# Empty rows of a sorted buffer written from 16 partitions and asked ahead of a weight load

## The chip, the cores and the metric

The kernel runs on one core of a Trainium2 chip. The metric is the device time of one launch in microseconds (us), taken as the median of several runs. The engines are named as the profile names them: PE is TensorE's matmuls, DVE is VectorE, ACT is ScalarE, POOL is GpSimd, SP is SyncE. Loads and stores are asked by SP's queue (q1) or by POOL's (q0); both are carried by the core's 16 DMA engines.

## What is computed

Three layers follow each other: an attention between 8 x 8 heads of 512 tokens and 32 state rows, a gated product layer, and a mixture of 8 experts with one expert for each token. Only the last matters here:

```python
def _moe2_ref(x, w_gate, w_output_gate, w1, w2):   # x: 4352 x 512 here
    logits = x @ w_gate
    e_idx = np.argmax(logits, axis=1)
    ...
    for e in range(E):                             # 8 experts
        mask = e_idx == e
        h = np.maximum(x[mask] @ w1[e], 0.0)       # 512 -> 1024
        ye = h @ w2[e]                             # 1024 -> 512
        out[mask] = gate_w[mask, None] * eom[mask, e, None] * ye
```

How many tokens an expert gets is known only on the chip. All matrix products are done with each operand split into a high and a low part.

## The kernel before

**Stages.** The first 700 us compute the first two layers, a group of 544 tokens at a time, and for each finished group the router's numbers. POOL then scatters the group's rows (L224) into a buffer in device memory, `ysort`, of 4 x 36864 rows of 130 numbers: 128 values, a gate, and the token's number. Each expert has its own stretch of rows in it, filled from the front; `cum` counts them. When the last 256 tokens are being computed, most rows are sorted, and the expert that has most of them (`eoh`, chosen by `choose`) is known, so two steps of 256 of its rows are run ahead of the others, in an order written out by hand in `moe_kernel`. Behind them comes a loop (`run`, L1278 on) whose steps are read from a table that the chip has made by then; every engine runs its own program in it, and all engines enter it together, when everything ahead of it is finished, transfers too.

**Empty rows.** A step works on 256 rows, or 128 for a half step's transfer, so the last step of an expert reads past its last row. What stands there must be harmless: zeros, with a number (`PADID`) beyond the last token, which makes the store leave the row out. `pads` (L1060) writes 128 such rows behind each expert's last row, and 128 more for the chosen expert, nine blocks in all, each into the four quarters of `ysort`. The places are in `pad`, worked out in `table` (L1135 to L1143). The source is `zrow`, one empty row on each of the 128 partitions.

**The order around it.** On SP's queue there stand, in the order of the source: the first two fetches of rows (`fetch_pre`), the load of the next expert's second weight into `raw2` (`load_rank`, L1093, which needs the expert's number from `rtab`), the nine writes of `pads`, and the third fetch (`fetch_pre(2)`), which reads `ysort` and so waits for every row written to it, by POOL or by `pads`. ACT and DVE split `raw2` into its high and low part in four quarters (`wsplit(1, raw2, c)`, L903 and L904) between their copies of the products' results (L964 relu copies, L970). Between the third and the fourth quarter DVE turns the third fetch's data (`turn(0)`, L946), and `parts` (L955, L961) splits it for the loop's first step. `pin` keeps the order of the source on PE, ACT, DVE and SP in this part.

**Stores.** The two steps ahead of the loop give their result to `preout` (L1054): DVE scales (L980), POOL writes rows by their token numbers (L990). Both stores of a step write to `out`; the scheduler knows no more of the places, so the second waits for the first. For writes that it is told are disjoint (`disjoint`, used by the scatter and by `pads`) it makes no such wait.

Of the kernel before, what the change touches and what calls it, by code (L numbers as in the profile page):

```python
# [8 lines left out]
F32 = mybir.dt.float32  # L9
F32R = mybir.dt.float32r  # L10
I32 = mybir.dt.int32
# [7 lines left out]
P = 128  # L19
# [14 lines left out]
RB = DM // 4 + 2  # L34
YW = 16 * RB
PADID = 1 << 20
# [774 lines left out]
ds = bass.ds  # L811
# [4 lines left out]
HB = 64  # L816
# [6 lines left out]
class Phase2:  # L823
# [82 lines left out]
    def tiles(self, ctx):  # L906
        tc, ph = self.tc, self.ph
        p = ctx.enter_context(tc.tile_pool(name="m1", bufs=1, reuse_waits="tile"))
        self.raw2 = p.tile([P, 4 * CH], F32, name="raw2")
        self.yT = p.tile([P, 4, 2, G], F32R, name="yT")  # L910
        self.hT = p.tile([P, 2, 2, 2, G], F32R, name="hT")
        self.hTB = self.hT.rearrange("p j f h n -> p (j f h n)").rearrange("p (c h n) -> p c h n", c=8, h=2)
        self.yts = p.tile([P, CH], F32, name="yts")
        self.hs = ph.srT.rearrange("p j n -> p (j n)")
        self.tab = p.tile([1, NSTEP, len(FIELDS)], I32, name="tab")
        self.zrow = p.tile([P, RB], F32, name="zrow")
        self.nc.gpsimd.memset(self.zrow[:, 0 : RB - 1], 0.0)
        self.nc.gpsimd.memset(self.zrow[:, RB - 1 : RB].bitcast(I32), PADID)
        self.ob = [ph.yTf[:, F2 + DM * i : F2 + DM * i + DM] for i in range(2)]
        bank = lambda pool, tag, n: pool.tile([P, 512], F32, tag=tag, name=n)  # L920
        self.ps_h = [bank(ph.ps_ab, "ab", f"ps_h{i}") for i in range(2)]
        self.ps_o = [bank(ph.ps_y, f"y{i}", f"ps_o{i}") for i in (2, 3, 0, 1)]
# [131 lines left out]
    def preout(self, k):  # L1054
        for t in range(2):
            self.gate(self.nc.vector, k, t)
            self.store(self.nc.gpsimd, k, t)

    def pads(self):

        nc = self.nc
        why = "table() bounds every field"
        _, rows = nc.values_load_multi_w_load_instructions(
            self.pad[0:1, 0 : NE + 1],
            engines=[nc.sync.engine],
            min_val=0,
            max_val=NE * CAP - P,
            skip_runtime_bounds_check_because=why,
        )
        for row in rows:  # L1070
            i = nc.sync.dma_start(
                out=self.ph.ysort[:, ds(row, P), :].rearrange("a p w -> p a w"),
                in_=self.zrow.unsqueeze(1).to_broadcast([P, 4, RB]),
            )
            self.ph.disjoint(i)

    def load(self, e, k, *names):

        why = "table() bounds every field"
        i = AT[names[0]]  # L1080
        lim = [LIMIT[n] for n in names]
        _, v = self.nc.values_load_multi_w_load_instructions(  # L1082
            self.tab[0:1, k, i : i + len(names)],
            engines=[e.engine],
            min_val=0,
            max_val=max(lim),
            skip_runtime_bounds_check_because=why,
        )
        return [
            self.nc.s_assert_within(x, int(n in ("rank1", "rank")), m, skip_runtime_bounds_check_because=why)  # L1090
            for x, m, n in zip(v, lim, names)
        ]
# [6 lines left out]
    def table(self, cp):  # L1099
# [6 lines left out]
        def t(shape, dt=F32):  # L1106
            n = 1
            for d in shape:
                n *= d
            o = tmp[:, free[0] : free[0] + n]  # L1110
            free[0] += n
            if len(shape) == 2:
                o = o.rearrange("p (a b) -> p a b", a=shape[0])
            return o.bitcast(dt)

        def iota(shape, pattern, base=0, cm=0):
# [10 lines left out]
            out=lt, in_=lt, pattern=[[1, NE], [-1, NE]], compare_op=ALU.is_gt, fill=0.0, base=0, channel_multiplier=0  # L1127
# [16 lines left out]
        self.fold = self.ph.tri[:, 0 : P // 2]  # L1144
        x, y = (self.ph.ident[:, P // 2 * i : P // 2 * i + P // 2] for i in range(2))
        nc.gpsimd.tensor_tensor(out=self.fold, in0=x, in1=y, op=ALU.add)

        yield
        V.scalar_tensor_tensor(out=cnt, in0=self.eoh, scalar=float(-G * NPRE), in1=cnt, op0=ALU.mult, op1=ALU.add)
# [15 lines left out]
        def red(o, i):  # L1165
# [3 lines left out]
            out=cmp, in0=key.unsqueeze(1).to_broadcast(sq), in1=key.unsqueeze(2).to_broadcast(sq), op=ALU.is_gt  # L1169
# [11 lines left out]
        er = pick(e8)  # L1181
        V.tensor_copy(out=self.rtab, in_=er)
        self.load_rank()
        self.pads()
        yield
        nr = pick(nb)
        gr = pick(ng)
# [19 lines left out]
        def total(o, v, scalar, op0, u=None):  # L1207
# [8 lines left out]
        rank, row, fst, lst, ex2, ex1, bsr, ngr, at, over = (t([1]) for _ in range(10))  # L1216
# [4 lines left out]
            out=later[:, 0:NE], in0=er, scalar=float(-NE), in1=ex[:, 0:NE], op0=ALU.add, op1=ALU.mult  # L1221
# [39 lines left out]
            out=own,  # L1261
# [8 lines left out]
            out=ps[:, 0:n], lhsT=self.ph.ones, rhs=own.rearrange("p k f -> p (k f)"), start=True, stop=True  # L1270
# [111 lines left out]
    def pool(self, guard):  # L1382
        e, s = self.nc.gpsimd, self.s

        def store(k):
            def both():
                for t in range(2):
                    e.wait_ge(s["o"], 2 * (k + 1) + t + 1)
                    self.store(e, k, t).then_inc(s["so"], 16)

            def half():

                e.wait_ge(s["so"], 32 * (k + 1))
                self.store(e, k, 1, HB, self.zrow[:, RB - 1 : RB]).then_inc(s["so"], 16)
                e.wait_ge(s["o"], 2 * (k + 2))
                self.store(e, k, 0, HB).then_inc(s["so"], 16)

            if k < 0:
                both()
                return  # L1400
            (kind,) = self.load(e, k, "half")
            with e.If(kind == 0):
                both()
            with e.Else():
                half()

        def fetch(k):
            half, row = self.load(e, k, "half", "row")
            if k > 3:
                e.wait_ge(s["tn"], k - 3)  # L1410

            def go(n):
                for d in self.fetch(e, self.yin[k % 3], self.gt[k % 4], row, n):
                    d.then_inc(self.sy[k % 3], 16)

            with e.If(half == 0):
                go(2)
            with e.Else():
                go(0)

        fetch(1)
        fetch(2)

        def step(k):
            store(k - 1)
            guard(k + 2, lambda: k and fetch(k + 2))

        def end(k):
            store(k)
            e.wait_ge(s["so"], 32 * (k + 2))  # L1430

        guard.run(step, end)
# [336 lines left out]
def moe_kernel(tc, x, state, w_a, w_b, w_out, w_gate, w_og, w1, w2, out):  # L1769
    w_a, w_b, w_out = (w.bitcast(I32) for w in (w_a, w_b, w_out))  # L1770
    with ExitStack() as ctx:
# [10 lines left out]
        w2 = lambda c: m.wsplit(0, m.raw1[:, 1], c)  # L1782
        turn = lambda i: m.turn(tc.nc.vector, m.yin[i])
        stage = lambda: next(table, None)
        turn(0)
        m.parts()
# [78 lines left out]
```

## Time and profile before

| | us |
|---|---|
| three runs | 1182.05, 1184.09, 1184.73 |
| median | 1184.09 |
| profiled execution | 1187.72 |
| its span | 1186.0 |
| PE busy | 1123.9 (95%) |
| DVE busy | 648.5 (55%) |
| ACT busy | 430.1 (36%) |
| POOL busy | 283.9 (24%) |

The profile is one execution; its span is the time between the first and the last instruction, and all moments below are counted from its start. A timeline has the start and the duration of an instruction, or of several alike (x4) from the first's start to the last's end; the brackets have how long the engine had been idle and what released it. A releaser called "issue" means that the profile shows none. The waits of a queue are totals, with their number and the longest. A row of a table by windows has the length of the window, the busy time of PE, PEld (weight loads), DVE, ACT and POOL, the clock that TensorE was granted (1.00 is full), the share of the 16 DMA engines that was busy (transfers can overlap, so it can pass 1) and the GB/s that they moved. Issues of DMA on SP are not busy time, and what a transfer costs from the ask to its landing stands in a list of its own.

### The profile page before, as it was taken

Reading aid. Unit: us, or ns where it says so; the run is one execution under the profiler, and the core shown is the slowest. Engines: PE = TensorE matmul, PEld = TensorE weight load, DVE = VectorE, ACT = ScalarE, POOL = GpSimd, SP = SyncE. Lnnn points to the kernel's source line nnn. Section 1 sums busy time; section 2 is a strip of 40 time slices with the busy share of each in tenths; the row PEclk is TensorE's granted clock in tenths of the full one; section 3 lists DMA queues with packets and bytes.
Section 4 is the critical chain, followed back from the end, with each engine's and each line's share of the span. In section 5 each row is a group of like instructions: output and inputs, shape, how many; then the busy total and the mean of one; then the engine's idle time right before and its main releaser. Section 6 shows DMA issues by size and latency. Waiting matters only on the chain. (4 is left out here: it accounts for less than half of the span.)

```text
span 1186.0 us, 19358 instructions
## 1 busy us (share of the span) xinstructions
PE 1123.9 (95%) x7032; PEld 902.4 (76%) x7032; DVE 648.5 (55%) x1118; ACT 430.1 (36%) x706; POOL 283.9 (24%) x392
## 2 busy tenths in 40 slices
PE   3898999999999999999999999969999999999994
PEld 1665777777677777776777799859899998889983
DVE  5889646565464465654754366742442444455463
ACT  4765424333333343333432245321421324142341
POOL 2000005006023050060230524311331232232121
PEclk8898999999999999999999999989999999999997
DMA  6563320302203103020000116369271253536420
GB/s 196 192 226 107 72 38 30 79 3 72 38 15 78 19 30 79 1 72 1 12 26 1 35 33 182 96 128 239 67 204 41 62 166 74 147 89 164 103 97 21
DMA packets 102497, 98.92 MB, mean 83 GB/s; under 512 B 60144, under 2 KB 76048, under 8 KB 102352
## 3 DMA queue, kind: packets, MB, share of 16 engines
q1 hardware_dynamic: 90920, 71.56, 23.2%
q0 software_dynamic: 11168, 25.52, 7.6%
q8 instruction: 72, 1.18, 0.4%
q14 instruction: 73, 0.60, 0.2%
q10 hardware_dynamic: 264, 0.07, 0.0%
HBM read 76.75 MB, written 21.15 MB: 83 GB/s over the span
## 5 line engine op out<-in xcount | busy, mean ns | idle before, releaser
L1009 PE MATMUL ps_h<-yT,w 128*128 128x256 f32 x1536 | 197.5, 285 | 11.0 <-issue 10.0
L1009 PEld LDWEIGHTS ps_h<-yT,w 128*128 128x128 f32 x1536 | 193.9, 193 | 16.8 <-issue 10.8
L1030 PE MATMUL ps_o<-w,hT 128*128 (+1 forms) x768 | 188.1, 394 | 2.3 <-DVE hT L970 2.2
L224 POOL DMA_INDIRECT ysort<-y,gdu x136 | 152.2, 1119 | 149.4 <-DVE y L797 105.8
L528 PE MATMUL ps_y<-gh,wo_h 128*128 128x512 f32 (+1 forms) x432 | 167.1, 392 | 2.1 <-ACT wo_h L218 1.9
L528 PE MATMUL ps_y<-gh,wo_l 128*128 128x512 f32 (+1 forms) x432 | 165.5, 383 | 0.1
L1030 PEld LDWEIGHTS ps_o<-w,hT 128*128 128x128 f32 x768 | 141.5, 190 | 29.8 <-issue 2.4
L528 PE MATMUL ps_y<-gl,wo_h 128*128 128x512 f32 (+1 forms) x432 | 163.3, 379 | 0.0
L516 PE MATMUL ps_ab<-Ah,Mh 128*128 128x512 f32 x384 | 129.6, 418 | 6.8 <-ACT Mh L258 6.8
L501 DVE TENSOR_TENSOR a<-a,ps_ab 128x512 f32<-128x512 f32 x96 | 65.6, 684 | 127.8 <-PE ps_ab L516 126.9
L516 PE MATMUL ps_ab<-Al,Mh 128*128 128x512 f32 x384 | 121.8, 398 | 0.0
L516 PE MATMUL ps_ab<-Ah,Ml 128*128 128x512 f32 x384 | 119.5, 392 | 0.0
L516 PEld LDWEIGHTS ps_ab<-Ah,Mh 128*128 128x128 f32 x384 | 66.7, 191 | 63.1 <-issue 40.2
L990 POOL DMA_INDIRECT out<-yT,gt x37 | 44.6, 1205 | 281.6 <-DVE yT L980 226.7
L964 ACT ACTIVATE hT<-ps_h 128x512 fp32r<-128x512 f32 x64 | 38.0, 593 | 201.5 <-PE ps_h L1009 194.1
L258 ACT ACTIVATE gh<-a 128x512 fp32r<-128x512 f32 (+1 forms) x108 | 65.4, 606 | 106.5 <-DVE a L501 106.5
L528 PEld LDWEIGHTS ps_y<-gh,wo_h 128*128 128x128 f32 x432 | 81.6, 189 | 26.5 <-issue 6.3
L259 DVE TENSOR_TENSOR gl<-a,gh 128x512 fp32r<-128x512 f32 (+1 forms) x108 | 71.1, 658 | 44.6 <-ACT gh L258 44.5
L970 DVE SCALAR_TENSOR_TENSOR hT<-ps_h,hT 128x512 fp32r<-128x512 f32 x64 | 44.0, 687 | 93.7 <-ACT hT L964 93.7
L500 ACT ACTIVATE a<-ps_ab 128x512 f32<-128x512 f32 x96 | 57.5, 599 | 101.4 <-PE ps_ab L516 101.2
L528 PEld LDWEIGHTS ps_y<-gl,wo_h 128*128 128x128 f32 x432 | 81.5, 189 | 16.3
L259 DVE TENSOR_TENSOR Ml<-ps_m,Mh 128x512 fp32r<-128x512 f32 x96 | 61.8, 684 | 56.5 <-ACT Mh L258 56.5
(255 smaller groups left out, 1410.7 us busy)
## 6 DMA issues: line engine op xcount, KB each, us to landing
raw<-in_moe_w SPq DMA_DIRECT2D x32, 512.0 KB, 10.1
raw<-in_moe_w SPq DMA_DIRECT2D x8, 2048.0 KB, 9.6
x<-in_x SPq DMA_DIRECT2D x7, 1024.0 KB, 5.5
xin<-in_x SPq DMA_DIRECT2D x96, 64.0 KB, 2.6
y<-in_moe_w_a SPq DMA_DIRECT2D x8, 512.0 KB, 5.8
yT<-in_moe_w_b SPq DMA_DIRECT2D x8, 512.0 KB
y<-ysort POOLq DMA_DIRECT2D x28, 128.0 KB, 8.6
y<-in_moe_w_out SPq DMA_DIRECT2D x6, 512.0 KB, 5.5
```

Source lines behind the costliest of these rows:

```text
L224: self.disjoint(self.nc.gpsimd.indirect_dma_start(**kw))
L258: self.nc.scalar.activation(out=hi, in_=src, func=AF.Copy)
L259: self.nc.vector.tensor_tensor(out=lo, in0=src, in1=hi.bitcast(F32), op=ALU.subtract)
L500: nc.scalar.activation(out=a[:, 0:n], in_=pa[:, 0:n], func=AF.Copy)
L501: nc.vector.tensor_tensor(out=a[:, 0:n], in0=a[:, 0:n], in1=pb[:, 0:n], op=ALU.mult)
L516: nc.tensor.matmul(out=ps, lhsT=m[:, ab, q, c0 : c0 + P], rhs=r[:, q, :], start=i == 0, stop=i == 5)
L528: nc.tensor.matmul(out=y, lhsT=l[:, f, P * c : P * c + P], rhs=r, start=f == 0 and i == 0, stop=f == NFC - 1 and i == 2,)
L964: return e.activation(out=self.hT[:, j % 2, :, 0, :], in_=self.ps_h[j % 2].rearrange("p (f n) -> p f n", f=2), func=AF.Relu)
L970: return e.scalar_tensor_tensor(out=l, in0=self.ps_h[j % 2].rearrange("p (f n) -> p f n", f=2), scalar=0.0, in1=h.bitcast(F32), op0=ALU.ma ...
L990: return e.indirect_dma_start(out=self.out, out_offset=bass.IndirectOffsetOnAxis(ap=to[0:rows].bitcast(U32), axis=0), in_=self.ob[t][0:row ...
L1009: m = e.matmul(out=self.ps_h[j % 2][:, G * (f % 2) : G * (f % 2) + G], lhsT=self.w1[:, wh, x : x + P], rhs=self.yT[:, c, yh, :], start=k == 0,
L1030: m = e.matmul(out=self.ps_o[2 * (k % 2) + t], lhsT=self.hT[:, j % 2, f, hh, P * t : P * t + P], rhs=self.w2c(slot, wh, 2 * j + f), start= ...
```

## The change

The empty rows get another source and another place in the queue, and two stores lose a wait.

- `tiles` makes no `zrow`. It clears the first 1040 columns of the first 16 partitions of `raw1`'s slot 0, which w1's splits are done with by then, and puts `PADID` into every 130th of them: 16 x 8 empty rows. A one-column `padid` takes over what the loop's half steps read from `zrow`.
- Each write of `pads` takes 8 rows in a run from each of 16 partitions, 64 pieces of 4160 bytes, where it took one row from each of 128, 512 pieces of 520 bytes.
- `pads` is called in `table` right behind the counts, one stage earlier, ahead of `load_rank`.
- `preout` tells the scheduler that its stores are disjoint.

```diff
@@ tiles
-        self.zrow = p.tile([P, RB], F32, name="zrow")
-        self.nc.gpsimd.memset(self.zrow[:, 0 : RB - 1], 0.0)
-        self.nc.gpsimd.memset(self.zrow[:, RB - 1 : RB].bitcast(I32), PADID)
+        self.padid = p.tile([P, 1], F32, name="padid")
+        self.nc.gpsimd.memset(self.padid.bitcast(I32), PADID)
+        self.empty = self.raw1[0:16, 0, 0 : 8 * RB]
+        self.nc.gpsimd.memset(self.empty, 0.0)
+        ids = self.empty.rearrange("p (r w) -> p r w", r=8)[:, :, RB - 1 : RB]
+        self.nc.gpsimd.memset(ids.bitcast(I32), PADID)
@@ preout
-            self.store(self.nc.gpsimd, k, t)
+            self.ph.disjoint(self.store(self.nc.gpsimd, k, t))
@@ pads
-                out=self.ph.ysort[:, ds(row, P), :].rearrange("a p w -> p a w"),
-                in_=self.zrow.unsqueeze(1).to_broadcast([P, 4, RB]),
+                out=self.ph.ysort[:, ds(row, P), :].rearrange("a (p r) w -> p a (r w)", p=16),
+                in_=self.empty.unsqueeze(1).to_broadcast([16, 4, 8 * RB]),
@@ table
         nc.gpsimd.tensor_tensor(out=self.fold, in0=x, in1=y, op=ALU.add)
+        self.pads()
 
         yield
...
         self.load_rank()
-        self.pads()
         yield
@@ pool, store, half
-                self.store(e, k, 1, HB, self.zrow[:, RB - 1 : RB]).then_inc(s["so"], 16)
+                self.store(e, k, 1, HB, self.padid).then_inc(s["so"], 16)
```

On SP's queue, between the second fetch and the third, this stood before (raw_6994 is `raw2`, raw_6148 is `raw1`; DMAHW0 to 7 are eight counters that the transfers of this queue take in turn, DMASW0 to 7 those of POOL's queue, and a transfer whose counter is still in use waits for it):

```order
L1096 TENSOR_LOAD rtab [waits DVE_49]
...
L894 DMA raw_6994<-in_moe_w 128x8x512 [waits DMAHW6_49,DVE_49]
L1063 TENSOR_LOAD pad
...
L1071 DMA ysort<-zrow 128x4x130 [waits DMAHW4_49,DMAHW3_49,DMAHW5_49,DMAHW2_49,DMAHW7_49,DMAHW1_49,Pool_49]
...
L1071 DMA ysort<-zrow 128x4x130 [waits DMAHW0_49]
...
L1071 DMA ysort<-zrow 128x4x130
...
L1071 DMA ysort<-zrow 128x4x130 [waits DMAHW6_49]
...
L1071 DMA ysort<-zrow 128x4x130 [waits DMAHW7_49]
L941 TENSOR_LOAD esel
...
L932 DMA y<-ysort 32x8x128 [waits DMAHW0_49,DMAHW7_49,DMASW1_49,DVE_49]
```

and this stands there now:

```order
L1066 TENSOR_LOAD pad [waits DVE_49]
...
L1074 DMA ysort<-raw_6148 16x4x1040 [waits DMAHW4_49,DMAHW5_49,DMAHW3_49,DMAHW6_49,DMAHW2_49,DMAHW7_49,DMAHW1_49,Pool_49]
...
L1074 DMA ysort<-raw_6148 16x4x1040
...
L1074 DMA ysort<-raw_6148 16x4x1040 [waits DMAHW0_49]
...
L1074 DMA ysort<-raw_6148 16x4x1040
...
L1074 DMA ysort<-raw_6148 16x4x1040 [waits DMAHW6_49]
L1099 TENSOR_LOAD rtab [waits DVE_49]
...
L894 DMA raw_6994<-in_moe_w 128x8x512 [waits DMAHW7_49,DVE_49]
L944 TENSOR_LOAD esel
...
L935 DMA y<-ysort 32x8x128 [waits DMAHW0_49,DMAHW6_49,DMASW1_49,DVE_49]
```

The nine writes have moved ahead of `raw2`'s load, whose counter is now the one of the second write (DMAHW7), so that it waits for that write's landing; the third fetch stays last.

On POOL, behind the last scatter of the group before and ahead of the rank sums of the last tokens (`cum`), the empty row is written. Before:

```order
L760 COPY y<-ids 128x8
L917 MEMSET zrow 128x129 [waits DVE_49]
L918 MEMSET zrow 128x1
L748 TENSOR_TENSOR cum<-cum,goh 128x8 [waits DVE_49,PE_49,Pool_49]
L747 COPY gpre<-cum 128x8 [waits Pool_49]
```

and now:

```order
L760 COPY y<-ids 128x8
L917 MEMSET padid 128x1 [waits DVE_49]
L919 MEMSET raw_6148 16x1040 [waits DMAHW3_49,DMAHW4_49,DMAHW2_49,DMAHW5_49,DMAHW1_49,DMAHW6_49,DMAHW0_49,DMAHW7_49,DVE_49,PE_49]
L921 MEMSET raw_6148 16x8 [waits Pool_49]
L748 TENSOR_TENSOR cum<-cum,goh 128x8 [waits DVE_49,PE_49]
L747 COPY gpre<-cum 128x8 [waits Pool_49]
```

The clearing now waits for SP's loads and for the splits of w1, since its place is a piece of `raw1`; its position on POOL is the same. The two early stores on POOL lie behind the scatters of the last tokens. Before:

```order
L1146 TENSOR_TENSOR tri<-ident 128x64 [waits PE_49]
L224 DMA ysort<-y,gdu 147456x130 [waits DMAHW4_49,DMAHW3_49,DMAHW5_49,DMAHW2_49,DMAHW6_49,DMAHW1_49,DMAHW7_49,DMASW2_49,DVE_49]
...
L224 DMA ysort<-y,gdu 147456x130 [waits DMASW1_49]
L990 DMA out<-yT,gt_6499 4352x512 [waits DMASW2_49,DMAHW0_49,DVE_49,Activation_49]
L990 DMA out<-yT,gt_6499 4352x512 [waits DMASW3_49,DMASW2_49,DVE_49]
```

and now:

```order
L1149 TENSOR_TENSOR tri<-ident 128x64 [waits PE_49]
L224 DMA ysort<-y,gdu 147456x130 [waits DMAHW4_49,DMAHW3_49,DMAHW5_49,DMAHW2_49,DMAHW6_49,DMAHW1_49,DMAHW7_49,DMASW2_49,DVE_49]
...
L224 DMA ysort<-y,gdu 147456x130 [waits DMASW1_49]
L993 DMA out<-yT,gt_6499 4352x512 [waits DMASW2_49,DVE_49,Activation_49]
L993 DMA out<-yT,gt_6499 4352x512 [waits DMASW3_49,DVE_49]
```

The second store no longer waits for the first (DMASW2), and the first no longer for a transfer of SP's queue (DMAHW0). On PE nothing moves, and on ACT and DVE only the counter of `raw2`'s load is another.

## Rows read from the trace of the kernel before

**Rows 1.** TensorE timeline: start us, us, line, operation, count, [idle before, releaser].

```profile
784.96 2.91 PE L1030 MATMUL ps_o<-w,hT 128*128 128x512 f32 x12
797.87 4.49 PE L1009 MATMUL ps_h<-yT,w 128*128 128x256 f32 x24 [10.00 <-issue]
```

**Rows 2.** Windows: us, PE, PEld, DVE, ACT, POOL, clock, DMA share, GB/s.

```profile
790.00:792.00 2.00, 0.00 (x0) 0.00 (x0) 0.89 (x1) 0.00 (x0) 0.00 (x0) 0.69 0.03 1
```

**Rows 3.** Waits of the SyncE queue, 720 to 800: total us, times, longest.

```profile
SPq L932 <- DMA ysort<-zrow: 7.3, 1, 7.3
SPq L1322 <- DVE w L904: 4.5, 1, 4.5
```

**Rows 4.** SyncE timeline: the w2 load, the empty rows, the third fetch.

```profile
761.68 0.40 SPq L894 DMA_DIRECT2D raw<-in_moe_w  x1
763.32 13.76 SPq L1071 DMA_DIRECT2D ysort<-zrow  x9
785.55 2.06 SPq L932 DMA_DIRECT2D y<-ysort  x4
```

**Rows 5.** VectorE timeline: counts, w2 splits (L904), copy (L970), turn (L946).

```profile
754.05 0.17 DVE L1143 CAST pad<-srT 128x9 int32<-128x9 f32 x1
777.08 1.21 DVE L904 TENSOR_TENSOR w<-raw,w 128x1024 fp32r<-128x1024 f32 x1
778.22 0.43 DVE L1272 CAST tab<-ps_tab 1x280 int32<-1x280 f32 x1
780.17 0.69 DVE L970 SCALAR_TENSOR_TENSOR hT<-ps_h,hT 128x512 fp32r<-128x512 f32 x1 [1.53 <-ACT hT L964]
781.12 2.36 DVE L904 TENSOR_TENSOR w<-raw,w 128x1024 fp32r<-128x1024 f32 x2 [0.26 <-ACT w L903]
791.11 1.25 DVE L946 STREAM_TRANSPOSE yts<-y 128x1024 f32<-128x1024 f32 x1 [7.63 <-DMA y<-ysort]
794.51 1.23 DVE L904 TENSOR_TENSOR w<-raw,w 128x1024 fp32r<-128x1024 f32 x1 [0.17 <-ACT w L903]
```

**Rows 6.** DMA issues: count, KB each, median us from ask to landing.

```profile
raw<-in_moe_w SPq DMA_DIRECT2D x8, 2048.0 KB, 9.6
ysort<-zrow SPq DMA_DIRECT2D x9, 260.0 KB, 10.2
```

**Rows 7.** Windows during empty rows, a 128-partition w2 load, a 32-partition w1 load.

```profile
775.00:776.00 1.00, 1.00 (x7) 0.86 (x6) 0.93 (x13) 0.00 (x0) 0.72 (x1) 1.00 1.23 183
...
882.00:883.00 1.00, 1.00 (x11) 1.00 (x10) 0.81 (x2) 0.00 (x0) 0.00 (x0) 1.00 1.07 410
...
948.00:949.00 1.00, 1.00 (x7) 0.84 (x6) 0.00 (x0) 0.82 (x1) 0.00 (x0) 1.00 1.06 205
```

**Rows 8.** SyncE line L1063: count, duration ns min, median, max.

```profile
L1063 SPq TENSOR_LOAD <-pad x1: 793/793/793, 762.1 to 762.1; - x1
```

**Rows 9.** POOL timeline: memset, rank sums, last scatter, second early store.

```profile
734.11 0.21 POOL L917 MEMSET zrow<- 128x129 f32 x1 [7.49 <-DVE wl L259]
751.42 0.20 POOL L748 TENSOR_TENSOR cum<-cum,goh 128x8 f32<-128x8 f32 x1 [17.07 <-DVE goh L733]
764.22 0.98 POOL L224 DMA_INDIRECT ysort<-y,gdu  x1 [0.30 <-issue]
785.07 0.98 POOL L990 DMA_INDIRECT out<-yT,gt  x1 [9.35 <-issue]
```

**Rows 10.** ScalarE timeline: first split of raw2, relu copies (L964).

```profile
773.64 1.05 ACT L903 ACTIVATE w<-raw 128x1024 fp32r<-128x1024 f32 x1
779.54 0.60 ACT L964 ACTIVATE hT<-ps_h 128x512 fp32r<-128x512 f32 x1 [4.85 <-PE ps_h L1009]
785.16 0.60 ACT L964 ACTIVATE hT<-ps_h 128x512 fp32r<-128x512 f32 x1 [3.12 <-PE ps_h L1009]
```

**Rows 11.** SyncE timeline in the loop: a w2 load, four w1 loads.

```profile
877.26 0.40 SPq L894 DMA_DIRECT2D raw<-in_moe_w  x1
944.42 1.82 SPq L897 DMA_DIRECT2D raw<-in_moe_w  x4
```


## The prediction

> **What bounds the kernel now.** I read four views of the seam between the hand-ordered steps and the last loop, in this order: TensorE's timeline for the hole, the waits of the SyncE queue for its cause, the timelines of SyncE, VectorE and ScalarE for the chain that ends it, and the DMA rates for what each load costs.
>
> [...] The reader sees "issue" as the releaser, which here is the common start of the loop on all engines. Who is last to it is told by the SyncE queue: it waits 4.5 us for VectorE's w at L904, and before that its fetch at L932 waits 7.3 us for the empty rows, ysort<-zrow [rows 3]. So the chain is: raw2 asked at 761.68, nine transfers of empty rows asked from 763.32 on over 13.76 us, the third fetch released at 785.55 [rows 4], its data turned by VectorE from 791.11, the last w2 split over at 795.74 (794.51 + 1.23) [rows 5], the loop at 797.87, which is 2.13 us later. Everything from the turn to the end of that split takes 4.63 us.
>
> The queue works in order, and sizes and rates reproduce this. A 2048 KB w2 load takes 9.6 us from ask to landing; nine times 260 KB are 2.40 MB of empty rows [rows 6]; while they run alone the DMA moves 183 GB/s [rows 7]. So 761.7 + 9.6 + 2.40 MB / 183 GB/s (13.1 us) = 784.4 against the release seen at 785.5. I use the same reckoning below.
>
> **The change part by part.**
>
> *The ask moves ahead.* The counts are in pad at 754.22 (754.05 + 0.17) [rows 5]. Loading them into registers takes SyncE 0.79 us [rows 8], and before the first transfer followed 1.2 us after that load began (763.32 against the end of raw2's issue at 762.08). So the first empty rows are asked at about 755.5, 7.8 us earlier. Nine issues go at the pace of the fetch (four in 2.06 us, about 0.55 us each with its register work) [rows 4], 5 us in all, hidden: SyncE has nothing else until the expert's number is known. What they read from, the cleared piece of raw1, is written on POOL inside its 17.07 us of idle time; the old memset of 129 columns took 0.21 us, eight times that at most here, 1.7 us [rows 9]. If that cover were gone, the pads would be later by those 1.7 us.
>
> *raw2 now stands behind them.* This is the price. raw2 is on the same queue, so its data comes after 2.40 MB of empty rows instead of ahead of them. ScalarE splits its first quarter at 773.64, and behind that split, in pinned order, stand the relu copy at 779.54, two more splits, and the copy at 785.16 [rows 10]; VectorE has its half of each, and only then the turn. While raw2 lands by about 778.7, all of that fits as it is. If it lands at L later than this, the path is: ScalarE 1.05 us for the first quarter and 0.1 to start, VectorE 1.21 + 0.43 + 0.69 + 2.36 less small overlaps (4.55) up to the turn, 4.63 to the end of the last split, 2.13 to the loop [rows 5, 10]. So the loop starts at L + 12.4, and break-even with 797.87 is L = 785.5.
>
> *The rate of the new transfers.* Nothing in the trace reads SBUF from 16 partitions in runs of 4160 bytes; I bound it. Loads of w1 go to 32 partitions at a time in pieces of 4 KB, and while four of them are alone in the queue (asked from 944.42 on) the DMA is fully busy and moves 205 GB/s; a w2 load to all 128 partitions, asked at 877.26, in pieces of 2 KB, moves 410 [rows 7, 11]. So with long pieces the number of partitions sets the rate: a quarter of them, half the rate. Upper end: 16 partitions are no worse than 32, 205 GB/s. Lower end: another halving, 102 GB/s. [...] Cost: 2.40 MB / 102 GB/s = 23.5 us against 13.1 before.
>
> [...]
>
> *Sum.* L = 755.5 + 23.5 + 9.6 = 788.6, loop at 801.0, 3.1 us later than before. [...] Everything in the loop hangs on its own progress, so it moves as a whole.
>
> *The third fetch.* It is asked when the empty rows have landed, about 783, its data comes behind raw2's, and VectorE gets to the turn only at L + 5.7 = 794.3. It is off the path now; the wait of 7.3 us goes, and raw2 is late in its place.
>
> *The early stores.* The second was held back until 785.07 [rows 9] by the first; it goes out at about 776. Neither store was last: the SyncE queue's last wait is for VectorE [rows 3]. Worth nothing here; if the loop could start at 791, the old order would have put its landing close to that, so it is a cover for the fast rival. The half steps read the id from the new padid column: same count and size, no cost. w1's next load into the cleared piece comes only in the loop.
>
> *Clock.* In the forecast TensorE idles from about 785 until VectorE's copy at L + 3.4, and again for over 4 us ahead of the loop; the trace shows the clock down after 2.9 us, so the loop's first group is at half clock as before. No term.
>
> **The rivals.**
>
> *Fast: 16 partitions carry 205 GB/s.* Then the pads take 11.7 us, raw2 lands at 776.8, the fetch before 781, VectorE turns at 783.48 (781.12 + 2.36), ScalarE's copy at 785.16 + 0.60 holds its split back by 1 us, the last split ends at 783.5 + 4.6 + 1.0 = 789.1, and the loop starts at 791.2, 6.6 us earlier: 1177.5. TensorE's hole is then 3.3 us, still past the 2.9 after which the clock fell, so I add no clock gain (1.6 us if it stays up: 1175.9). It holds from 176 GB/s up (13.6 us). For it: short pieces of 520 bytes ran at only 183 with the engines fully busy, so length matters too. [...] Against it: the 205 to 410 above.
>
> *Middle: 117 to 176 GB/s*, when reading out of SBUF is held back less than writing into it. Between the break-even and the full gain the end goes in proportion; at 140 GB/s 17.1 us, L = 782.2, loop at 794.6, 3.3 us gained: 1180.8.
>
> [...]
>
> [...]
>
> **How the numbers follow.** The profiled execution took 1187.72 us, its span 1186.0, so 1.7 us lie outside; the seam moves inside the span. Its own sum is 1187.7 + 3.1 = 1190.8; the profiled execution is 3.6 us above the median of the three runs, 1184.09, and I carry the difference over to that median: 1187.2. Forecast (95 to 117 GB/s) 0.60, its own range 1184.5 to 1190.5; fast 0.24; middle 0.12; worse 0.04. A measurement of this kernel can tell about 0.2%, 2.4 us, from no change. Of the forecast 0.42 is slower by more and 0.18 within; the middle gives 0.07 faster and 0.05 within; worse is slower. Together slower 0.46, within 0.23, faster 0.31. As the fast case holds more than 2 in 10, the range reaches to it: 1177.0 to 1190.5.
>
> **What would show it.** In the profile after: the transfers ysort<-raw asked at 755 to 761 in nine issues of some half a microsecond; the DMA rate near 100 GB/s from 757 until about 780 with full busy shares; ScalarE's first L903 on raw2 waiting for the DMA until about 788; TensorE idle twice, from 785 and ahead of the loop; no wait of the fetch on the pads that VectorE feels. What would make it wrong: a rate near 200 in that stretch, ScalarE's split still at 774, the turn at 783.5. Then the fast rival holds, and the partition count does not bind transfers out of SBUF.

## The result and the profile after

The changed kernel takes 1191.08 us (median of six runs, 1187.91 to 1195.23), the kernel before 1183.30 in the six runs beside it (1180.94 to 1184.73): a ratio of 1.0070 with a 95% interval of 1.0045 to 1.0095. It is slower, by some 8 us where 3.1 were forecast, and the median lies 0.6 us above the range's upper end.

The profiled execution of the changed kernel took 1187.91 us, its span 1186.2, so beside the 1186.0 of before nothing seems to have happened. Two things in single executions hide the loss. The early part ran 3.18 us faster in this one: the cast of the counts, VectorE's L1143 at 754.05 before [rows 5], now L1146, starts at 750.87. And from the loop's first matmul to the end it took 383.5 us instead of 388.1; the execution of before lost time there in two stretches, of which these are the windows (us, busy of PE, PEld, DVE, ACT, POOL, granted clock, DMA share, GB/s):

```profile
989.87:1021.87 32.00, 29.80 (x180) 26.67 (x179) 18.69 (x23) 14.00 (x20) 11.23 (x14) 0.96 0.49 109
1021.87:1053.87 32.00, 32.00 (x191) 28.50 (x191) 11.96 (x16) 7.91 (x13) 5.17 (x7) 0.98 0.31 101
```

TensorE loses 2.2 us and then runs below full clock in both; the windows of after at the same distance from the loop's start show 31.94 and 32.00 busy at 1.00. What made the loss is open. That execution was the one that stood 3.6 us above its median. So I compare the seam alone, **from the start of the counts' cast to the loop's first matmul**: 43.8 us before (754.05 to 797.87), 51.9 after (750.87 to 802.72), 8.0 us more, which is the 0.7% of the medians. To set a moment of after beside one of before, 3.18 us are to be added.

TensorE's timeline after (start us, us, line, operation, count, idle before and its releaser) answers [rows 1]:

```profile
778.91 3.03 PE L1012 MATMUL ps_h<-yT,w 128*128 128x256 f32 x24
792.14 1.22 PE L1033 MATMUL ps_o<-w,hT 128*128 128x512 f32 x2 [10.19 <-ACT hT L967]
793.86 3.92 PE L1033 MATMUL ps_o<-w,hT 128*128 128x512 f32 x10 [0.49 <-DVE hT L973]
802.72 5.03 PE L1012 MATMUL ps_h<-yT,w 128*128 128x256 f32 x24 [4.95 <-issue]
```

One hole of 10 us has become two, of 10.2 and 5.0. The first waits for ScalarE's relu copy, which stands behind ScalarE's first split of `raw2`. ScalarE, then VectorE's first split, turn and last split, answering [rows 10] and [rows 5]:

```profile
790.54 1.06 ACT L903 ACTIVATE w<-raw 128x1024 fp32r<-128x1024 f32 x1 [19.96 <-DMA raw<-in_moe_w]
...
791.63 1.23 DVE L904 TENSOR_TENSOR w<-raw,w 128x1024 fp32r<-128x1024 f32 x1 [17.64 <-ACT w L903]
...
796.00 1.23 DVE L949 STREAM_TRANSPOSE yts<-y 128x1024 f32<-128x1024 f32 x1
...
799.39 1.23 DVE L904 TENSOR_TENSOR w<-raw,w 128x1024 fp32r<-128x1024 f32 x1 [0.17 <-ACT w L903]
```

ScalarE sits idle for 20 us, on a DMA. The turn, which waited 7.63 us for the third fetch before, waits for nothing. The queue's timeline and waits (total us, times, longest) answer [rows 4] and [rows 3]:

```profile
752.30 22.23 SPq L1074 DMA_DIRECT2D ysort<-raw  x9
777.31 0.42 SPq L894 DMA_DIRECT2D raw<-in_moe_w  x1
781.09 2.63 SPq L935 DMA_DIRECT2D y<-ysort  x4
...
SPq L1325 <- DVE w L904: 7.3, 1, 7.3
SPq L935 <- DMA ysort<-raw: 1.4, 1, 1.4
```

The fetch's wait for the empty rows went from 7.3 us to 1.4. In its place `raw2` is asked at 777.31 where it was asked at 761.68, because the nine writes ahead of it hold SyncE for 22.23 us. Windows of two microseconds, answering [rows 7]:

```profile
755.00:757.00 2.00, 2.00 (x18) 1.92 (x17) 1.73 (x10) 0.00 (x0) 1.39 (x3) 1.00 1.01 125
773.00:775.00 2.00, 1.96 (x15) 1.66 (x14) 0.99 (x2) 0.00 (x0) 0.83 (x1) 1.00 1.02 98
777.00:779.00 2.00, 2.00 (x11) 1.64 (x10) 0.00 (x0) 0.00 (x0) 0.00 (x0) 1.00 1.01 245
783.00:785.00 2.00, 0.00 (x0) 0.00 (x0) 0.00 (x0) 0.00 (x0) 0.00 (x0) 1.00 1.03 375
787.00:789.00 2.00, 0.00 (x0) 0.00 (x0) 0.00 (x0) 0.00 (x0) 0.00 (x0) 0.50 0.93 140
```

Between 773 and 775 the empty rows' transfers (the pads, as they are called from here on) are alone, the scatters having landed by 772.0 and the first store's data starting at 774.96: the DMA counts as fully busy and moves 98 GB/s, against 183 for the old rows [rows 7]. `raw2` alone gets 375. The rest of the transfer detail in this text comes from the trace's single DMA packets: 576 of 4160 bytes, median 638 ns, from 753.29 to 780.35, against 4608 of 520 bytes, 35 ns, from 770.18 to 784.82 before.

### The profile page after: what moved, and what is told of

The parts are those of the page before. It is cut to its first block, busy times and chain, and to the rows that moved or that the text cites. A ratio compares the mean times of both kernels' runs of the same rounds, so it can differ in the third digit from the quotient of the medians.

```text
span 1186.2 us, 19363 instructions
## 1 busy us (share of the span) xinstructions
PE 1121.1 (95%) x7032; PEld 900.2 (76%) x7032; DVE 647.7 (55%) x1118; ACT 430.2 (36%) x706; POOL 284.1 (24%) x393
## 5 line engine op out<-in xcount | busy, mean ns | idle before, releaser
L1033 PE MATMUL ps_o<-w,hT 128*128 (+1 forms) x768 | 188.7, 395 | 10.8 <-ACT hT L967 10.2
```

The lines of the kernel that those rows point to most:

```text
L1033: m = e.matmul(out=self.ps_o[2 * (k % 2) + t], lhsT=self.hT[:, j % 2, f, hh, P * t : P * t + P], rhs=self.w2c(slot, wh, 2 * j + f), start= ...
```

## Experiments

The theory after the result: sixteen neighbouring partitions give a transfer out of SBUF about 100 GB/s whatever else is done, and `raw2` behind it carries the delay to the loop. Rivals: the place ahead of `raw2` costs by itself; the long runs are slow by their size; the stores that no longer wait make the stretch longer. All twelve runs were on chips on which both kernels are 2.5 to 2.9% slower than in the runs above, and ScalarE waits once, for 7 to 9 us, inside the seam for something the profile calls remote; what that is stays open. Each ratio is therefore to the kernel before on the same chip in the same set, and none is compared with the 1191.08. e6c, e7, e9 and e10 ran on another chip than the other eight. The kernel before has no trace on either; e4, which has its order and its rows, stands in for it, and all lengths in us are of one execution each.

| kernel | pads: partitions, bytes a packet | packet, median ns | pads' stretch us | cast to raw2's first split | cast to loop | time against before (95%) |
|---|---|---|---|---|---|---|
| before, first runs | 128, 520 | 35 | 14.6 | 19.6 | 43.8 | 1 |
| changed, first runs | 16 neighbours, 4160 | 638 | 27.1 | 39.7 | 51.9 | 1.0070 (1.0045–1.0095) |
| e4 (order of before) | 128, 520 | 42 | 17.5 | 24.7 | 46.2 | 1.0006 (0.9977–1.0036) |
| e5b (changed again) | 16 neighbours, 4160 | 638 | 27.2 | 39.9 | 52.1 | 1.0049 (1.0025–1.0073) |
| e5 | 16 neighbours, 4160 | 638 | 26.2 | 39.2 | 51.4 | 1.0052 (1.0018–1.0086) |
| e9 | 16 neighbours, 4160 | 639 | 25.7 | 37.1 | 49.3 | one execution |
| e3, behind raw2 | 16 neighbours, 4160 | 639 | 22.8 | 24.4 | 50.4 | 1.0022 (0.9981–1.0063) |
| e1, e1b | 128, 520 | 34, 28 | 20.8, 22.2 | 31.9, 33.4 | 44.1, 45.5 | 0.9967 (0.9925–1.0009), 0.9981 (0.9958–1.0003) |
| e2 | 16, every 8th, 4160 | 304 | 13.7 | 24.6 | 41.8 | 0.9970 (0.9938–1.0003) |
| e7 | 32 neighbours, 2080 | 167 | 13.5 | 25.1 | 41.6 | one execution |
| e6, e6c | 32, every 4th, 2080 | 88, 88 | 9.4, 9.1 | 26.4, 25.4 | 43.6, 42.6 | 0.9983 (0.9955–1.0010), 0.9963 (0.9930–0.9996) |
| e10, behind raw2 | 32, every 4th, 2080 | 89 | 7.6 | 23.2 | 40.4 | 0.9974 (0.9947–1.0001) |

The seam of e5b is 5.9 us longer than that of e4, which is the 0.5% of its ratio. The split of the sixth column does not always wait for `raw2`: where it comes 28 us behind the cast or earlier, `raw2` has landed 1 to 8 us before it, and ScalarE's own order decides (in e7 ScalarE still waits 0.57 us for it).

**Form and place, one without the other.** The place alone, with the old rows (both kernels the same, in two sets):

```diff
...
-                in_=self.empty.unsqueeze(1).to_broadcast([16, 4, 8 * RB]),
...
+                in_=self.zrow.unsqueeze(1).to_broadcast([P, 4, RB]),
```

> The kernel after, but the empty rows again come from zrow, one row of 520 bytes from each of 128 partitions; they still stand ahead of raw2's load. Theory (the 16 neighbouring partitions set the rate): the rows go at 183 GB/s as before, 13.1 us from 755.5 on, raw2 lands near 779 instead of 790 (the trace after), the turn stands at its early place, the loop starts near 791 to 793 on the clock of the trace before: 5 to 6.6 us under the kernel before, about 1177 to 1178.5. Rival (the new order by itself costs, whatever the rows look like): raw2 is late by the whole transfer, and the time stays at or above the kernel before, 1183 or more.

> The move alone again (old rows of 128 partitions and one row, asked ahead of w2, stores no longer waiting for each other), on this set's chip. If the form makes the loss and not the place: within 0.3% of the kernel before or faster, 44 us or less from the cast to the loop, 7 to 10 us less than the changed kernel. If the place makes the loss (w2's raw half behind the pads): slower than before by 0.2 to 0.5%.

The form alone, with `self.pads()` back behind `self.load_rank()`:

> The kernel after, but pads is asked at its old place, behind raw2's load. Theory: raw2 is early again (ScalarE's first split of it at 774), but the rows take 24 to 27 us from 770 on, the third fetch is released near 797, and the loop starts near 809, 11 to 13 us later than before: 1194 to 1196. Rival (it is the order that costs): the time goes back to the kernel before, 1183.

The place alone shows no loss: 0.9967 and 0.9981, neither distinct from no change, with the loop 44.1 and 45.5 us behind the cast against 46.2 in e4. It delays ScalarE's first split of `raw2` by 7 to 9 us against e4, and the earlier third fetch pays for that: VectorE's turn comes 37.4 us behind the cast in e1 and 39.4 in e4. The starts of the loop in e4 and e1:

```profile
829.19 4.55 PE L1009 MATMUL ps_h<-yT,w 128*128 128x256 f32 x24 [7.55 <-issue]
...
832.39 4.61 PE L1011 MATMUL ps_h<-yT,w 128*128 128x256 f32 x24 [5.84 <-issue]
```

The gain of 5 to 6.6 us that I expected of e1 did not come, nor did its 13.1 us of pads, nor e1b's 44 us. Old rows that took 14.6 and 17.5 us behind `raw2` took 20.8 and 22.2 ahead of it, where the scatters run beside them.

The form alone has `raw2` early (24.4) and still starts the loop at 50.4, 4.2 us behind e4: the third fetch then waits for the pads, and VectorE's turn with it.

```profile
832.25 1.25 DVE L949 STREAM_TRANSPOSE yts<-y 128x1024 f32<-128x1024 f32 x1 [9.72 <-DMA y<-ysort]
```

I had expected a loop 11 to 13 us late and 0.9 to 1.1% of time. Its time, 1.0022, is not distinct from no change, so the seam of one execution is the evidence here, not the time. So the slow form delays the loop in either place, by a different wait: the fetch's behind `raw2`, `raw2`'s own ahead of it. That it costs time is shown for the place ahead alone.

**Which partitions.** Same place, same 64 pieces of 4160 bytes a write, but every eighth partition:

```diff
-        self.empty = self.raw1[0:16, 0, 0 : 8 * RB]
...
+        src = self.raw1[:, 0, 0 : 8 * RB]
+        self.nc.gpsimd.memset(src, 0.0)
...
+        self.empty = self.raw1[0:128:8, 0, 0 : 8 * RB]
```

> The kernel after, but the 16 partitions that the rows are read from are every eighth one (0, 8, ..., 120) instead of 0 to 15; transfers have the same shape, 16 x 4 pieces of 4160 bytes. Theory (neighbouring partitions share a way out of SBUF): nearer to 200 GB/s than to the 100 of the trace after, a packet of 4160 bytes near 0.3 us instead of 0.64, 12 to 13 us for all, time near 1177 to 1179. Rival (the number of partitions or the long piece sets the rate, not where they lie): 100 GB/s as after, time near 1191. [...]

Then 32 partitions, every fourth (`0:128:4`) or the first 32 (`0:32`), in runs of 4 rows:

> The changed kernel with the empty rows in 32 partitions, every fourth one, in runs of 4 rows (2080 bytes) instead of 16 neighbours in runs of 8; as many bytes. If the stretch goes by which partitions are read: every eighth of sixteen took 304 ns for 4160 bytes and 13.7 us in all, so every fourth takes 160 ns or less for 2080 bytes, 8 to 13.7 us in all; w2's raw half then lands early enough that the order's other end decides, and the time is 0.5 to 0.9% under the changed kernel and 0 to 0.4% under the one before. If the stretch goes by the size of a run: packets of half the size lie between the 14.6 us of 520 bytes and the 27 us of 4160 bytes, 17 to 24 us in all, and the time lies between the two kernels.

> The changed kernel with the rows in partitions 0 to 31, runs of 4 rows (2080 bytes). Against e6 only the choice of the partitions differs, against the changed kernel the count of neighbours. If neighbours share a way out of the memory, as sixteen neighbours at 638 ns for 4160 bytes and sixteen apart at 304 ns have it, thirty-two neighbours give the rate of sixteen apart: 140 to 165 ns for 2080 bytes, 12.5 to 15 us in all. If the size of a packet decides: 88 ns and 9.4 us, as in e6.

Windows of e3 (16 neighbours), e2 (16 apart), e7 (32 neighbours) and e6 (32 apart) while the pads run; in the last three some scatters run too:

```profile
813.00:817.00 4.00, 4.00 (x25) 3.54 (x24) 3.79 (x18) 1.05 (x2) 1.96 (x2) 1.00 0.97 100
...
784.00:787.00 3.00, 2.92 (x16) 2.26 (x16) 2.11 (x3) 0.00 (x0) 2.39 (x3) 1.00 0.95 221
...
787.00:791.00 4.00, 3.92 (x25) 3.30 (x24) 3.14 (x7) 0.00 (x0) 3.18 (x3) 1.00 0.98 212
...
786.00:788.00 2.00, 2.00 (x19) 2.00 (x18) 1.81 (x7) 0.00 (x0) 1.39 (x3) 1.00 1.00 305
```

Only the choice of partitions differs between the changed kernel and e2 (POOL clears the piece of `raw1` in all of them, long before): the packet takes 304 ns instead of 638, and the stretch halves. Only that choice differs between e7 and e6: 167 ns, just above the 140 to 165 expected, and 88 ns. The time per byte is nearly the same for 16 apart (304 ns for 4160 bytes, 0.073 ns a byte) and 32 neighbours (167 for 2080, 0.080). So among these forms neither the size of a run nor the number of partitions as such sets the rate. The first 16 stand at 0.153 ns a byte and every fourth of 128 at 0.042, one step above those two and one below: reading 16 apart instead of as neighbours is worth a factor of 2.1 (638 to 304 ns), reading 32 apart one of 1.9 (167 to 88 ns). Why neighbours are slower, no run shows.

The DMA counts as 0.95 to 1.00 busy in all four. The times follow: e5b's interval, 1.0025 to 1.0073, lies above those of e2 (0.9938 to 1.0003) and e6 (0.9955 to 1.0010). The gain of e2 over the kernel before, about 0.5% as I expected it, is 0.3% and not clear of none.

The old rows do not fit into these steps alone: they come from all 128 partitions and take 14.6 to 17.5 us behind `raw2`, where 32 apart take 7.6 (e10). Their packets are a quarter as long as e10's and four times as many; no run separates that from the partitions.

**The stores.** The two stores' old wait back in the changed kernel, the change of the stores alone in the kernel before, and the stores left out of the changed one:

```diff
-            self.ph.disjoint(self.store(self.nc.gpsimd, k, t))
+            self.store(self.nc.gpsimd, k, t)
```

> The changed kernel with the two early stores waiting for each other again; nothing else is edited. If the stores' share of the pads' stretch is what made it longer than the 23.5 us that I forecast: the second store falls behind the first's landing, so one of the two leaves the pads' stretch or meets only its end, the stretch gets 1 to 2 us shorter, the loop begins 1 to 2 us earlier, and the time is 0.1 to 0.2% under that of the changed kernel. If sixteen neighbouring partitions alone set the stretch (its packets went at 23 to 24 a us outside the stores' two dips as well): the stretch, the loop's start and the time stay within 0.1% of the changed kernel.

> The kernel before with one line of the change: the two early stores are told to be disjoint. Theory: the second store leaves near 776 instead of 785, nobody waits for it, time within 0.2% of the kernel before. Rival: the two stores at once slow the empty rows or the third fetch, which are on the path, by their 0.5 MB: up to 2.5 us slower.

> The changed kernel without the two early stores (their output rows are left out), to see what of the pads' stretch is theirs. With nothing beside them the same pads took 22.75 us behind w2's raw half; ahead of it, beside the scatters and the stores, 27.1 and 27.2; with one store beside them 26.2. If scatters and stores make up the difference: 25 to 25.6 us here, and w2's raw half lands 1.5 to 2.5 us earlier from the cast than in the changed kernel. If the stretch is longer because of something else ahead of w2: 27 us again.

In the order of before the stores' wait shows in no time (1.0006, 0.9977 to 1.0036). In the changed kernel both stores together take 1.5 us of the pads' stretch (e5b's 27.2 against e9's 25.7, where I expected 25 to 25.6) and 2.8 us of the seam, by one trace each from two chips; chaining them again gives back 1.0 of the stretch, as expected, 0.7 of the seam, a little less than expected, and no time that can be measured, 1.0052 against 1.0049. They are not the main cause: without them the pads still take 25.7 us, and the loop still starts 3.1 us later behind the cast than in e4, which has both stores.

**The changed kernel once more, and a better one.**

> The changed kernel once more, unedited, so that its trace stands beside those of this set from one chip. Expected: slower than the kernel before by 0.5 to 0.9%; pads' packets near 638 ns, 26 to 28 us from the first to the last; from the start of the cast at which the pads are asked to the loop's first matmul 51 to 53 us (51.9 in its first trace, 43.8 in the trace of the kernel before).

> Thirty-two partitions, every fourth, ahead of w2's raw half, once more and in five rounds, since three left its gain unclear (0.9983, 0.9955 to 1.0010). If the loop's start is what the form buys (43.6 us from the cast to the loop against 52.1 in the changed kernel on the same chip, 46.2 with the old rows and order): 0.2 to 0.4% faster than the kernel before, the interval clear of 1. If the earlier loop start is given back later: within 0.1% of the kernel before.

> The same form of the rows asked at the old place, behind w2's raw half; with e6c this tells the place apart from the form. w2's raw half then lands as early as in the kernel before, and the pads, 9.4 us instead of 14.6 to 17.5, let the third fetch go 5 us earlier or more. If a pads' stretch of that length no longer matters wherever it stands: 41.5 to 44 us from the cast to the loop, within 0.2% of e6c. If the place counts by itself: 45 us or more, and slower than e6c by over 0.2%.

On the first of the two chips the changed kernel is 0.5% slower than the kernel before, with the same stretch and the same packets as in its first trace. The form of e6 and e6c beats the kernel before in e6c, 0.9963 with the interval just clear of 1; the same kernel in e6 gave 0.9983, which is not. e10 has the same form at the old place, and the loop starts 40.4 us behind the cast, 1.1 earlier than the least I expected and 2.2 earlier than in e6c; ScalarE's wait for "remote" is 7.2 us there and 9.4 in e6c, which is all of that difference. Its time, 0.9974, cannot be told from e6c's. With a quick form the place matters little: the hole ahead of the loop is 3.2 us in both, in e6c and e10:

```profile
828.00 4.47 PE L1013 MATMUL ps_h<-yT,w 128*128 128x256 f32 x24 [3.23 <-issue]
...
820.07 4.61 PE L1013 MATMUL ps_h<-yT,w 128*128 128x256 f32 x24 [3.24 <-issue]
```

## Why the prediction was right in direction and short in size

The chain was the right one. Moments in the clock of the trace of before (after plus 3.18):

| step | forecast | found | miss so far |
|---|---|---|---|
| pads asked | 755.5 | 755.5 | 0 |
| their last packet | 779.0 | 783.5 | +4.5 |
| raw2 at ScalarE (L) | 788.6 | 793.7 | +5.1 |
| loop's first matmul | 801.0 | 805.9 | +4.9 |

The median, 1191.08, misses the forecast of 1187.2 by 3.9 us and not by 4.9, mostly because six runs put the kernel before at 1183.30, where I had counted from 1184.09.

**The ask** came when I said. **The path from L to the loop**, 12.4 in the forecast, took 12.2 (790.54 to 802.72). **The rate** was right too: in the undisturbed middle of e3's stretch, and at the end of those ahead of `raw2`, 48 packets end in each two microseconds, 99.8 GB/s, against my estimate of 102, a halving of the 205 [rows 7] that no row of before showed. The fast and the middle rival fall, and with them the 205 GB/s as an upper end: the first 32 partitions gave about that in e7 (212), the first 16 half of it (98 to 100). The reason that I gave for the rate was only half right. I had it halve with the number of partitions; e2 reads 16 and moves 221 GB/s, some scatters included. What halves it is which 16 they are, neighbours or not, and for that the forecast had no price.

**The term that failed is the pads' 23.5 us**, which is 28.1 from the ask (752.30 to 780.35). It was bytes over rate alone, with nothing for the start or for what runs beside the pads, and there it went wrong. The first packet runs 1.0 us behind the ask. At 24 packets a microsecond the 576 need 24.0 us, 0.5 more than forecast. The scatters cost 1.7 us: in e9, which has no stores, 344 packets end in the first 16 us, when the scatters run, instead of 384, and its stretch is 25.7. The rest up to 27.1, 1.4 us, is the stores', whose earlier issue the forecast put at nothing; e5b less e9 gives 1.5. Together 4.6 us: the whole of the pads' miss, and nearly all of the 4.9 us by which the loop is late against the forecast.

**raw2 gained nothing behind the pads.** I had the nine issues down for 5 us, at the pace of the fetch, with SyncE free from 761 on and `raw2`'s command waiting in the queue; yet the same nine issues had taken 13.76 us before [rows 4]. The views of the lines L1074, the nine issues, and L1099, the load of the expert's number into a register (duration in ns: least, median, most; first and last start), after, and of the latter, L1096, before:

```profile
L1074 SPq DMA_DIRECT2D ysort<-raw x9: 321/2727/3447, 752.3 to 771.9; - x9
...
L1099 SPq TENSOR_LOAD <-rtab x1: 2193/2193/2193, 774.6 to 774.6; - x1
...
L1096 SPq TENSOR_LOAD <-rtab x1: 278/278/278, 760.9 to 760.9; - x1
```

The median issue took 2.7 us, as long as the DMA needs to work off one such transfer (64 packets at 24 a microsecond). And the register load, a single number, took 2.19 us where it had taken 0.28; e3, which has it ahead of the pads, shows 0.28 too, e5, e5b and e9, which have it behind them, 1.28, 1.90 and 2.08. So `raw2` was asked only 3.0 us before the pads' last packet. That was enough to hide its start-up: its first packet starts at 779.18, 1.9 us behind the ask and 1.2 us before the pads' last one ends. What this gained went again at the other end, and ScalarE had `raw2` 10.2 us behind the pads instead of 9.6. Its last tenth trails: 90% of its packets have ended by 785.74, the last at 789.82 (before: 770.00 and 771.36). The third fetch's packets run beside that tail, but they do so in e2 and e7 too, from about the same point of `raw2`'s data on, and the last tenth takes 1.2 and 1.6 us there instead of 4.1. So the fetch alone does not make it; what does is open.

**The third fetch, the clearing and the stores' order** went as said: the turn did not wait for the fetch, POOL's clearing (0.95 us at 738.12) was long done, and the stores' earlier issue brought no gain. **The clock** was put at nothing. TensorE's granted clock fell to 0.50, the lower of the two levels (1.00 and 0.50) that the traces of before and after show, at 786.5 in the first hole, rose to 1.00 at 796.8 in the work between the holes, and stood at 0.50 again from 800.2, in the second hole, to 807.0. The loop's first group took 5.03 us against 4.49 [rows 1], since it ran at the lower level for its first 4.3 us against 3.1 before; this half microsecond lies behind the seam. The clock went down 4.6 us behind the last matmul ahead of the first hole and 2.4 behind that ahead of the second, so the 2.9 of the trace before (787.87 to 790.77), by which I judged the holes, is no fixed figure.

The chance "worse", later than the forecast, had 0.04, and that was too little: other traffic beside the pads, which the sum left out, is what the runs show as most of the miss, 3.1 us of it (scatters 1.7, stores 1.4). How it slows them is not shown; the old rows, from all 128 partitions, grew longer beside the same scatters too (20.8 and 22.2 us against 14.6 and 17.5). I took such sharing as an extreme, where the scatters and two stores were already known to run near that stretch.

## What to carry to other kernels

Which partitions a transfer out of SBUF read set what it got here: sixteen neighbours gave 98 to 100 GB/s, a third of the 305 of 32 spread over all 128 (some scatters included), for the same bytes. The old rows, 520-byte packets from all 128 partitions, came between the two at 183 [rows 7]. A transfer that moves ahead of another on a queue in order must be priced with everything that runs beside it and with the time that its issues hold the issuing engine, since what stands behind it is asked later: here 3.1 us of traffic, and 22.2 us of SyncE with `raw2` asked at 777.31 instead of 761.68. Before moving a transfer off a wait, see what the one that is moved back feeds: here 5.9 us less of the fetch's waiting (7.3 to 1.4) was paid with 20 us of ScalarE's waiting for `raw2`.

## What the runs showed of the hardware

- A fully busy DMA is no sign of work at full rate: shares of 0.97 to 1.03 stand beside 98 and 100 GB/s (16 neighbours), 212 (32 neighbours), 305 (32 apart) and 375 (`raw2`) in the windows above.
- Nine issues of 260 KB held SyncE for 22.2 us with sixteen neighbours, for 13.8 with the old rows behind `raw2` [rows 4] and 9.8 and 9.4 with them ahead of it (e1, e1b), and for 9.8 with 32 apart.
- A load of one number into a register of SyncE took 1.3 to 2.2 us behind the pads of sixteen neighbours (four traces), and 0.28 ahead of them or behind the old rows of e1.
- The first 16-neighbour packets behind `raw2` in e3 went much faster, 100 in two microseconds with some of 161 ns, before the rate settled at 48. I have no explanation for that.
